# Transposing the MLP's rows by DMA instead of on TensorE, two blocks ahead, and preparing the recurrence's first operands a block earlier

## The chip, the cores and the metric

The kernel runs on one core of a Trainium2 chip. The metric is the device time of one execution in microseconds (us), the median of several. The engines named below are TensorE (PE; PEld is its weight load), VectorE (DVE), ScalarE (ACT), GpSimd (POOL) and SyncE (SP), which issues most DMAs. Each runs its own instructions in order and waits for others by semaphores.

## What is computed

Two parts share the input `x` (2048 rows of 512, bf16) and are mixed by a gate. Part A is attention over segments of 32 rows with 8 memory rows that each segment passes on to the next, so its 64 segments are a chain. Part B is a layer norm and an MLP (512 to 1376 to 512) on each row.

```
g = sigmoid((x * gate_w).sum(-1))
# A, for each segment s of 32 rows, H = 32 heads of 128:
h = concat([mem, x[s]]);  q, k, v = h @ Wq, h @ Wk, h @ Wv
o = softmax(mask(q @ k.T * scale)) @ v @ Wo;  mem = o[:8];  a[s] = o[8:]
# B:
y = (x - mean) / sqrt(var + eps)
b = gelu(y @ w1 + b1) @ w2 + b2
return g * a + (1 - g) * b
```

## The kernel before

The kernel is written under a manual schedule: each engine executes its instructions in the order in which the program emits them, and the tile framework adds the waits. A tile of a pool with `bufs=n` takes the buffer of the n-th tile before it, and its first write waits until all readers of that one are done, also those that the program emits later on another engine.

The MLP comes first (about the first 97 us), and the loop over the 64 segments (L646) after it. The weights of part A are loaded while the MLP runs.

The MLP goes over 8 blocks (`NBLK`) of 2 x 128 rows and, in each, over 11 chunks of the hidden width (`FC`). The list `units` (L504) has all (block, chunk) pairs, and the loop at L505 emits for each:

- `a_mm` (L456): four PE matmuls of a w1 chunk with the transposed rows `yT` into one of two PSUM banks (SbF and W in turn), then ACT's Gelu (L461) out of that bank into `hTm`.
- `b_mm` (L463), two units behind (`LAG`): two PE matmuls of `hTm` with w2, which sum over the chunks in banks U[0], U[1] for even blocks and U[2], U[3] for odd ones. After the last chunk ACT scales the two sums by `omg` = 1 - g into `ct` (L473), and POOL issues their stores to `c_dr` (L476).
- between them, by the chunk number, the side work:
  - chunk 0: `gates(blk - 1)` (L447): ACT's tanh of `z_all` (L449), then on DVE `g_all` and `omg` (L450, L451). Then `prep(blk + 1)` (L414) on DVE: mean and variance of the two row tiles (L420, L421), an inverse square root by Newton steps (`rsqrt`), and the normalised rows `y` (L432), in two buffers.
  - chunks 6 and 7 (7 and 8 in block 0): `prep_tr` (L435), for one row tile each: four PE transposes of `y` into bank X1 or X2 (L439), and a DVE copy to `yT` (L440).
  - chunk 7 (8 in block 0): `gate_sums` (L442) on DVE: the sums of x * gate_w of the block's two tiles into `z_all`. It is the last reader of the row tiles `xt`.
  - chunk 8: `loads(blk)` (L339) on SP: two tiles of x, which take the buffers that `gate_sums(blk)` frees (6 buffers), then two pieces of 1 MB of Wv, Wq or Wk. In block 3 it also loads `xT` of the first two tiles, by a transposing DMA from DRAM (L94), and the memory rows `m0`. Block 6 adds Wo.
  - chunk 9: a part of the constants (`consts`, L377) on DVE.

In the last block, part A's first work is mixed in by the generator `first` (L478): PE transposes of `m0` and a DVE copy to `hT[0]`, POOL copies of the left rows of tiles 0 and 1 (`left_x`, L97, into `GL`) and of `hT[0]` (`prep_h`, L235), and then 24 units of projection matmuls that read `GL` (`left_v`, `left_qk`). The numbers at L534 say how many steps of it each chunk takes.

What stands in an engine's order ahead of what matters below. On ACT: the Gelu of a(b,0), the tanh of block b-1, the Gelu of a(b,1), the two `ct` of block b-1, the Gelu of a(b,2). On POOL: the stores of `ct`, then, in the last block, `GL`. On SP: the x tiles, then the weight pieces.

Of the kernel before, what the change touches and what calls it, by code (L numbers as in the profile page):

```python
# [10 lines left out]
BF16 = mybir.dt.bfloat16  # L11
# [16 lines left out]
def kernel(ctx, tc, A_x, A_mem0, A_Wq, A_Wk, A_Wv, A_Wo, A_seg_len, B_x, B_w1, B_b1, B_w2, B_b2, gate_w, out):  # L28
    nc = tc.nc
    P = 128  # L30
    _, S, Dm = A_x.shape
# [6 lines left out]
    KC = Dm // P  # L38
# [8 lines left out]
    RIDE = 32 - M  # L47
# [23 lines left out]
    hT = [ep.tile([P, KC, 32], BF16, name=f"hT{i}") for i in range(3)]  # L71
# [20 lines left out]
    def load_xT(T):  # L92
        xT = ew.tile([P, KC, P], BF16, tag="xT", bufs=3, name="xT")
        nc.sync.dma_start_transpose(out=xT[:], in_=x2[T * P:(T + 1) * P, :])  # L94
        xTs[T] = xT

    def left_x(T):  # L97
        GL = ew.tile([P, KC, LEFT, SPT], BF16, tag="GL", name="GL")
        nc.gpsimd.tensor_copy(out=GL[:].rearrange("p k c i -> p k i c"), in_=xTs[T][:].rearrange("p k (i t) -> p k i t", i=SPT)[:, :, :, RIDE:seg])
        GLs[T] = GL  # L100
# [56 lines left out]
    dve_q, act_q = [], []  # L157

    def flush(q, n=1):
        for _ in range(min(n, len(q))):  # L160
            q.pop(0)()
# [4 lines left out]
    def left_qk(T, t, hf, bk):  # L166
        for kc in range(KC):
            qk_unit(bk, gl(T), t, hf, kc)
            if kc < KC - 1:
                yield  # L170
        def ca():
            Tb = qk_cast(bk[:])
            dve_q.append(lambda: qk_tr(Tb, QL[T % 2], hf) if t == 0 else kl_tr(Tb, T, hf))
        act_q.append(ca)
        yield
# [6 lines left out]
    def left_v(T, vb, bk):  # L182
        if vb == 0:
            VLs[T] = ew.tile([P, 4, 2, Dh], BF16, tag="VL", bufs=1, name="VL")
        for kc in range(KC):
            v_unit(bk, gl(T), vb, kc)
            if kc < KC - 1:
                yield

        def ca():  # L190
            VL = VLs[T]
            nc.scalar.copy(out=VL[:, :, vb, :], in_=bk[:].rearrange("p (a e) -> p a e", a=4))

            if vb == 1:
                vp_load(T, 0)
        act_q.append(ca)
        yield
# [37 lines left out]
    def prep_h(s):  # L235
        T, si = divmod(s, SPT)
        nc.gpsimd.tensor_copy(out=hT[s % 3][:, :, 0:RIDE], in_=xTs[T][:, :, seg * si:seg * si + RIDE])
# [54 lines left out]
    with tc.tile_pool(name="mlpw", bufs=1) as mlpw, \  # L292
         tc.tile_pool(name="mwork", bufs=2) as mwork, \
         tc.tile_pool(name="msmall", bufs=2) as msmall:
        TB = 2
        NBLK = NT // TB
# [9 lines left out]
        def ld_x(T, eng=nc.sync):  # L306
            xt = mwork.tile([P, Dm], BF16, tag="xt", bufs=6, name="xt")
            eng.dma_start(xt[:], x2[T * P:(T + 1) * P, :])
            xts[T] = xt

        def ld_w(W_, A, n):
            nc.sync.dma_start(W_[:, n, :], A[n * P:(n + 1) * P].rearrange("p h e -> p (h e)"))

        def ld_o(i):
            nc.sync.dma_start(Wo_sb[:, i:i + 8, :], A_Wo[i:i + 8].rearrange("h e d -> e h d"))
# [23 lines left out]
        def loads(blk):  # L339
            if 2 * blk + 7 < NT:  # L340
                ld_x(2 * blk + 6)
                ld_x(2 * blk + 7)
            if blk == 3:
                for T in range(2):
                    load_xT(T)
                nc.sync.dma_start(m0[:], A_mem0[0])

            for kc in range(2 * blk, min(2 * blk + 2, 3 * KC)):
                ld_w(*((Wv_sb, A_Wv), (Wq_sb, A_Wq), (Wk_sb, A_Wk))[kc // KC], kc % KC)
            if blk == 6:  # L350
                for i in range(0, H, 8):
                    ld_o(i)
# [49 lines left out]
        def rsqrt(y, v, n):  # L402
            i1 = msmall.tile([P, n], I32, tag="i1", name="i1")
            nc.vector.tensor_scalar(out=i1[:], in0=v.bitcast(I32), scalar1=1, scalar2=None, op0=ALU.logical_shift_right)
            nc.vector.tensor_scalar(out=y.bitcast(I32), in0=i1[:], scalar1=-1, scalar2=RSQRT_SEED, op0=ALU.mult, op1=ALU.add)
            for _ in range(3):
                t = msmall.tile([P, n], FP32, tag="nt", name="nt")
                nc.vector.tensor_tensor(out=t[:], in0=y, in1=y, op=ALU.mult)
                nc.vector.scalar_tensor_tensor(out=t[:], in0=t[:], scalar=-0.5, in1=v, op0=ALU.mult, op1=ALU.mult)
                nc.vector.scalar_tensor_tensor(out=y, in0=t[:], scalar=1.5, in1=y, op0=ALU.add, op1=ALU.mult)  # L410

        ys, yTs = {}, {}

        def prep(blk):  # L414
            mv = msmall.tile([P, TB, nc.vector.BN_AGGR_DIM], FP32, tag="mv", name="mv")
            ve = msmall.tile([P, TB], FP32, tag="ve", name="ve")
            rs = msmall.tile([P, TB], FP32, tag="rs", name="rs")
            for tt in range(TB):
                st = msmall.tile([P, nc.vector.BN_STATS_DIM], FP32, tag="st", name="st")
                nc.vector.bn_stats(out=st[:], in_=xts[blk * TB + tt][:])  # L420
                nc.vector.bn_aggr(out=mv[:, tt, :], in_=st[:])  # L421
            nc.vector.tensor_scalar(out=ve[:], in0=mv[:, :, 1], scalar1=LN_EPS, scalar2=None, op0=ALU.add)
            if blk == 0:
                nc.scalar.activation(out=rs[:], in_=ve[:], func=ACTF.Sqrt)
                nc.scalar.activation(out=dummy[:], in_=ident[:, 0:1], func=ACTF.Gelu_apprx_tanh)
                nc.vector.reciprocal(out=rs[:], in_=rs[:])
            else:
                rsqrt(rs[:], ve[:], TB)
            for tt in range(TB):
                T = blk * TB + tt  # L430
                ys[T] = mwork.tile([P, Dm], BF16, tag="y", name="y")
                nc.vector.tensor_scalar(out=ys[T][:], in0=xts[T][:], scalar1=mv[:, tt, 0:1], scalar2=rs[:, tt:tt + 1], op0=ALU.subtract, op1=ALU.mult)  # L432
            yTs[blk] = mwork.tile([P, KC, TB * P], BF16, tag="yT", name="yT")

        def prep_tr(blk, tt):  # L435
            y, bk = ys.pop(blk * TB + tt), (X1, X2)[tt]
            tp = bk[:].bitcast(BF16)[:, 0:Dm].rearrange("p (k t) -> p k t", k=KC)
            for kc in range(KC):
                nc.tensor.transpose(tp[:, kc, :], y[:, kc * P:(kc + 1) * P], ident[:])  # L439
            nc.vector.tensor_copy(out=yTs[blk][:, :, tt * P:(tt + 1) * P], in_=tp)  # L440
# [34 lines left out]
                        nc.vector.tensor_scalar(out=ct[:], in0=bp(blk, tt)[:], scalar1=omg[:, T:T + 1], scalar2=None, op0=ALU.mult)  # L475
                    (nc.gpsimd if blk < NBLK - 1 else nc.sync).dma_start(c_dr[T * P:(T + 1) * P, :], ct[:])  # L476

        def first():  # L478
            m0p = X1[:].bitcast(BF16)[:, 0:KC * M].rearrange("p (k m) -> p k m", k=KC)
            for kc in range(KC):  # L480
                nc.tensor.transpose(m0p[:, kc, :], m0[:, kc * P:(kc + 1) * P], ident[:M, :M])
            dve_q.append(lambda: nc.vector.tensor_copy(out=hT[0][:, :, RIDE:32], in_=m0p))
            for T in range(2):
                left_x(T)
            prep_h(0)
            yield
            bks = (X1, X2, U[0], X1, X2, U[0])
            for n, (v, t, hf) in enumerate(((1, 0, 0), (1, 0, 1), (0, 0, 0), (0, 1, 0), (0, 0, 1), (0, 1, 1))):
                yield from (left_v(0, hf, bks[n]) if v else left_qk(0, t, hf, bks[n]))
# [15 lines left out]
        for n, (blk, fc) in enumerate(units):  # L505
            a_mm(blk, fc)
            if n == len(units) - 1:
                dummy = msmall.tile([P, 1], FP32, tag="dummy", name="dummy")
                nc.scalar.activation(out=dummy[:], in_=omg[:, 0:1], func=ACTF.Exp)
            if n >= LAG:  # L510
                b_mm(*units[n - LAG])
            if fc == 0:
                if blk >= 1:
                    gates(blk - 1)
                if blk + 1 < NBLK:
                    prep(blk + 1)
                else:
                    gate_sums(blk)
            if blk + 1 < NBLK:
                f0 = 7 if blk == 0 else 6  # L520
                if fc in (f0, f0 + 1):
                    prep_tr(blk + 1, fc - f0)
                if fc == f0 + 1:
                    gate_sums(blk)
                if fc == 8:
                    loads(blk)
                if fc == 9:
                    next(cgen, None)
            elif fc >= 1:
                if fc == 1:  # L530
                    side0 = first()
                if fc == 3:
                    gates(blk)
                for _ in range((0, 1, 1, 0, 0, 8, 0, 8, 0, 8, 0)[fc]):  # L534
                    next(side0, None)
                    flush(act_q, 9)
                    flush(dve_q, 9)
# [363 lines left out]
```

## Time and profile before

| what | value |
|---|---|
| median of 3 runs | 787.48 us (785.29 to 788.54) |
| the profiled execution | 785.75 us, span 784.0 us |
| granted TensorE clock | 0.998 |
| HBM read and written | 56.96 MB and 4.45 MB |
| DMA, mean over the span | 90 GB/s |
| TensorE idle for POOL's `GL` (L99) in the last block | 1.5 us |

The span is the time from the first to the last instruction of the profile; the execution's own time is 1.75 us longer. Busy time of an engine counts each instruction from start to end; PE's matmuls overlap, so that the distance from one start to the next is what a matmul costs. Rows of a timeline give start, duration, engine, line, operation, output and inputs, the number of instructions merged, and in brackets the idle time before and what ended it.

### The profile page before, as it was taken

The page shows a single profiled execution, that of the slowest core. Times are in us where ns is not written, and L with a number is a line of the kernel's source. Part 1 is how long each engine was busy: PE and PEld are TensorE (multiplying, and loading weights), DVE is VectorE, ACT ScalarE, POOL GpSimd, SP SyncE. Part 2 cuts the span into 40 slices and gives each one's busy share as a digit, 9 for nine tenths or more (in the row PEclk, how much of TensorE's full clock was granted, in tenths as well). Part 3 has the DMA queues.
Part 4 walks back from the last instruction along what each step waited for, and adds up shares of the span by engine and source line. Part 5 has one row for each costly group of instructions (what it writes and reads, how often), then busy time and mean ns, then how long its engine had stood idle before and what let it go on. Part 6 is the DMA issues. An engine that isn't in the chain of part 4 may idle for free.

```text
span 784.0 us, 44302 instructions
## 1 busy us (share of the span) xinstructions
PE 766.3 (98%) x19673; PEld 416.6 (53%) x19687; DVE 341.2 (44%) x1235; ACT 524.5 (67%) x1439; POOL 278.8 (36%) x523
## 2 busy tenths in 40 slices
PE   7999999999999999999999999999999999999996
PEld 5666455555555555555555555555555555555553
DVE  5776244334334343434443433434343444434334
ACT  4666566667677676667667677766666767666663
POOL 4111034333344343344434424443334443342342
PEclk9999999999999999999999999999999999999999
DMA  6789311213121222212121212122221212221211
GB/s 199 271 256 387 119 57 61 74 61 88 61 61 62 78 71 77 72 58 74 49 88 61 88 62 74 60 67 70 78 72 57 80 43 88 62 80 62 67 63 44
DMA packets 53174, 70.61 MB, mean 90 GB/s; under 512 B 21289, under 2 KB 42898, under 8 KB 51442
## 3 DMA queue, kind: packets, MB, share of 16 engines
q1 hardware_dynamic: 51250, 64.84, 25.6%
q8 instruction: 156, 2.56, 1.3%
q0 software_dynamic: 784, 1.97, 0.7%
q10 hardware_dynamic: 944, 0.92, 0.4%
q14 instruction: 40, 0.33, 0.1%
HBM read 56.96 MB, written 4.45 MB: 78 GB/s over the span
## 4 chain that ended last, share of the span: by engine, by line
PE 87%; DVE 1%; issue 0%; ACT 0%; DVEq 0%
PE U L120 30%; PE X L139 18%; PE W L151 15%; PE X L120 7%; PE X L151 4%; PE U L281 3%; PE U L640 2%; PE U L268 1%; PE W L257 1%; PE SbF L257 1%; PE W L249 1%; PE SbF L600 1%; PE SbF L249 1%; PE U L286 1%; PE U L466 1%; PE U L221 0%
## 5 line engine op out<-in xcount | busy, mean ns | idle before, releaser
L626 POOL TENSOR_TENSOR UT<-XR,Rb 128x384 bf16<-128x384 bf16 x126 | 140.3, 1134 | 297.6 <-DMA Rb<-r_dr 237.6
L125 ACT CAST Tb<-U 128x512 bf16<-128x512 f32 x258 | 150.9, 585 | 86.6 <-PE U L120 85.6
L120 PEld LDWEIGHTS <-hT 128*32 128x32 bf16 x4096 | 98.3, 96 | 110.9 <-DVE hT L642 26.8
L139 PE MATMUL X<-Wv_sb,hT 128*32 128x512 bf16 x2048 | 145.7, 379 | 0.0
L120 PE MATMUL U<-Wq_sb,hT 128*32 128x512 bf16 x2048 | 139.9, 381 | 0.8 <-DVE hT L642 0.5
L120 PE MATMUL U<-Wk_sb,hT 128*32 128x512 bf16 x2048 | 132.7, 379 | 0.0
L151 PE MATMUL W<-Wo_sb,UT 128*32 128x512 bf16 x2080 | 124.8, 380 | 1.5 <-ACT UT L718 1.5
L642 DVE CAST hT<-U 128x16 bf16<-128x16 f32 x126 | 22.0, 175 | 222.7 <-PE U L640 222.4
L129 DVE STREAM_TRANSPOSE QT<-Tb 128x256 f32<-128x256 f32 x128 | 56.6, 443 | 78.4 <-ACT Tb L125 78.4
L151 PEld LDWEIGHTS <-UT 128*32 128x32 bf16 x2080 | 57.8, 96 | 57.7 <-issue 18.5
L606 ACT CAST XR<-U 128x256 bf16<-128x256 f32 x252 | 78.6, 438 | 0.0
L129 DVE STREAM_TRANSPOSE KT<-Tb 128x256 f32<-128x256 f32 x128 | 57.1, 446 | 44.5 <-ACT Tb L125 44.3
L633 ACT CAST w<-W 128x256 bf16<-128x256 f32 (+1 forms) x128 | 41.9, 378 | 46.5 <-PE W L151 46.5
L139 PEld LDWEIGHTS <-hT 128*32 128x32 bf16 x2048 | 53.1, 95 | 20.4
L618 POOL TENSOR_TENSOR racc<-racc,R 128x72 f32<-128x72 f32 x63 | 21.2, 336 | 111.7 <-PE U L286 79.3
L626 POOL TENSOR_TENSOR UL<-XR,Rb 128x128 bf16<-128x128 bf16 x126 | 60.3, 502 | 0.0
L718 ACT CAST UT<-U 128x64 bf16<-128x64 f32 x252 | 35.3, 227 | 28.3 <-PE U L286 28.3
L710 ACT CAST V<-X 128x512 bf16<-128x512 f32 x64 | 37.4, 585 | 22.3 <-PE X L139 22.1
L466 PE MATMUL U<-w_sb,hTm 128*128 128x512 bf16 (+1 forms) x163 | 49.2, 379 | 0.6
L696 ACT CAST V<-X 128x512 bf16<-128x512 f32 x64 | 37.4, 585 | 15.6 <-PE X L139 15.6
L460 PEld LDWEIGHTS <-w_sb 128*128 128x128 bf16 (+1 forms) x352 | 34.2, 101 | 20.3 <-issue 3.0
L640 PEld LDWEIGHTS <-w 128*32 128x32 bf16 x1008 | 20.7, 94 | 42.6 <-ACT w L633 29.3
(158 smaller groups left out, 1179.8 us busy)
## 6 DMA issues: line engine op xcount, KB each, us to landing
Rb<-r_dr SPq DMA_DIRECT2D x63, 512.0 KB, 3.8
Wv_sb<-in_A_Wv_dram SPq DMA_DIRECT2D x4, 1024.0 KB, 6.5
Wq_sb<-in_A_Wq_dram SPq DMA_DIRECT2D x4, 1024.0 KB, 7.0
Wk_sb<-in_A_Wk_dram SPq DMA_DIRECT2D x4, 1024.0 KB, 9.5
Wo_sb<-in_A_Wo_dram SPq DMA_DIRECT2D x4, 1024.0 KB, 15.0
VP<-VL SPq DMA_DIRECT2D x64, 64.0 KB, 3.2
c<-c_dr SPq DMA_DIRECT2D x16, 128.0 KB, 3.3
out_dram<-o SPq DMA_DIRECT2D x16, 128.0 KB, 2.1
```

The source lines that it names most:

```text
L120: nc.tensor.matmul(bk[32 * j:32 * j + 32, :], lhsT=G[:, kc, :], rhs=W5[t][:, kc, h0:h1, j, :], start=(kc == 0), stop=(kc == KC - 1), tile_ ...
L125: nc.scalar.copy(out=Tb[:], in_=bk.rearrange("p (a b e) -> p a e b", a=8, b=2))
L129: nc.vector.transpose(out=dst[:, 8 * hf:8 * hf + 8, c0:c0 + 32, :].rearrange("p a r b -> p a (r b)").bitcast(FP32), in_=Tb[:].rearrange("p ...
L139: nc.tensor.matmul(bk[32 * j:32 * j + 32, :], lhsT=G[:, kc, :], rhs=Wv5[:, kc, 4 * vb:4 * vb + 4, j, :], start=(kc == 0), stop=(kc == KC - ...
L151: nc.tensor.matmul(bk[32 * c:32 * c + 32, :], lhsT=U_[:, j, i, :], rhs=Wo_sb[:, 4 * i + j, :], start=(n == 0), stop=(n == NW - 1), tile_po ...
L466: nc.tensor.matmul(bp(blk, tt)[:], lhsT=hTm[blk % 2][:rows, fc, tt * P:(tt + 1) * P], rhs=w2_sb[:rows, fc, :], start=(fc == 0), stop=(fc = ...
L606: nc.scalar.copy(out=XR[:, j], in_=U[j][:, 0:NG * 40].rearrange("p (i q) -> p i q", q=40)[:, :, 0:32])
L626: nc.gpsimd.tensor_tensor(out=out[:, :, 4 * h:4 * h + 4, o:o + b - a], in0=XR[:, :, 4 * h:4 * h + 4, a:b], in1=Rb[:, h, :, :, a:b], op=ALU ...
L633: nc.scalar.copy(out=w[:, a:a + Dm // parts], in_=W[:, a:a + Dm // parts])
L640: nc.tensor.matmul(bk[32 * c:32 * c + 32, M * k:M * k + M], lhsT=w[:, k * P + 32 * c:k * P + 32 * c + 32], rhs=SelM[:], start=(k == k0), s ...
L696: nc.scalar.copy(out=v_out(V, 0), in_=X1[:])
L710: nc.scalar.copy(out=v_out(V, 1), in_=X2[:])
```

## The change

For blocks 2 to 7, `yT` is no longer made by PE transposes and a DVE copy. SP issues a transposing DMA for each row tile, from `y` in SBUF to `yT` in SBUF (`dma_tr`). For this `prep` runs two blocks ahead: `prep(1)` at chunk 0 of block 0 and `prep(2)` at its chunk 8, ahead of `gate_sums(0)`; from block 1 on `prep(blk + 2)` at chunk 0. `dma_tr` of block 2 stands at chunks 1 and 3 of block 1, that of blocks 3 to 7 at chunk 7 of the block two before, ahead of `gate_sums` and `loads`. `yT` gets a third buffer; `y` keeps two. Blocks 0 and 1 keep the PE transposes.

The beginning of `first` (transposes of `m0`, `GL` of two tiles, `hT[0]`) becomes a function `first_h`, called at chunk 4 of block 6, with the DVE copy at once. `first` begins with the projection matmuls, and the numbers of steps for chunks 1 and 2 become 0.

```
             else:
                 rsqrt(rs[:], ve[:], TB)
+            yTs[blk] = mwork.tile([P, KC, TB * P], BF16, tag="yT", bufs=3, name="yT")
             for tt in range(TB):
...
-            yTs[blk] = mwork.tile([P, KC, TB * P], BF16, tag="yT", name="yT")
+
+        def dma_tr(blk, tt):
+            nc.sync.dma_start_transpose(out=yTs[blk][:, :, tt * P:(tt + 1) * P], in_=ys.pop(blk * TB + tt)[:])
...
-        def first():
+        def first_h():
             m0p = X1[:].bitcast(BF16)[:, 0:KC * M].rearrange("p (k m) -> p k m", k=KC)
             for kc in range(KC):
                 nc.tensor.transpose(m0p[:, kc, :], m0[:, kc * P:(kc + 1) * P], ident[:M, :M])
-            dve_q.append(lambda: nc.vector.tensor_copy(out=hT[0][:, :, RIDE:32], in_=m0p))
+            nc.vector.tensor_copy(out=hT[0][:, :, RIDE:32], in_=m0p)
             for T in range(2):
                 left_x(T)
             prep_h(0)
-            yield
+
+        def first():
             bks = (X1, X2, U[0], X1, X2, U[0])
...
-                if blk + 1 < NBLK:
-                    prep(blk + 1)
-                else:
+                if blk == 0:
+                    prep(1)
+                elif blk + 2 < NBLK:
+                    prep(blk + 2)
+                elif blk + 1 == NBLK:
                     gate_sums(blk)
             if blk + 1 < NBLK:
-                f0 = 7 if blk == 0 else 6
-                if fc in (f0, f0 + 1):
-                    prep_tr(blk + 1, fc - f0)
-                if fc == f0 + 1:
+                if blk == 0 and fc in (7, 8):
+                    prep_tr(1, fc - 7)
+                if 0 < blk and blk + 2 < NBLK and fc == 7:
+                    for tt in range(TB):
+                        dma_tr(blk + 2, tt)
+                if blk == 0 and fc == 8:
+                    prep(2)
+                if blk == 1 and fc in (1, 3):
+                    dma_tr(2, (fc - 1) // 2)
+                if fc == (8 if blk == 0 else 7):
                     gate_sums(blk)
                 if fc == 8:
                     loads(blk)
+                if blk == NBLK - 2 and fc == 4:
+                    first_h()
                 if fc == 9:
                     next(cgen, None)
...
-                for _ in range((0, 1, 1, 0, 0, 8, 0, 8, 0, 8, 0)[fc]):
+                for _ in range((0, 0, 0, 0, 0, 8, 0, 8, 0, 8, 0)[fc]):
```

## The prediction

> **What bounds the kernel now.** I read the page first, then the engines in order of time over the first 100 us, where the MLP and the whole change lie.
>
> ```profile
> span 784.0 us, 44302 instructions
> PE 766.3 (98%) x19673; PEld 416.6 (53%) x19687; DVE 341.2 (44%) x1235; ACT 524.5 (67%) x1439; POOL 278.8 (36%) x523
> POOL c_dr L476 <- ACT ct L473: 66.4, 7, 12.3
> PE X L139 <- POOL GL L99: 1.5, 1, 1.5
> ```
>
> TensorE is busy for 98% of the span, so only what TensorE does, or waits for, counts. The last row, from the waits of the first 100 us, is its one long wait there. The profiled execution took 785.75 us, the median shown is 787.48; I work in the first and add the difference in time to the second. About 0.5% (3.9 us) is what a measurement of this kernel can tell from no change. Below, a(b,f) is `a_mm` of block b, chunk f.
>
> **What goes.** Block 2 starts at 28.43, block 3 at 38.56, with two groups of PE transposes (L439) between them.
>
> ```profile
> 24.08 0.59 PE L466 MATMUL U<-w_sb,hTm 128*128 128x512 bf16 x2
> 24.51 0.39 PE L439 MATMUL X<-ident,y 128*128 128x128 bf16 x4
> 24.73 0.60 PE L460 MATMUL SbF<-yT,w_sb 128*128 128x256 bf16 x4
> ...
> 28.43 0.60 PE L460 MATMUL SbF<-yT,w_sb 128*128 128x256 bf16 x4
> ...
> 31.48 0.59 PE L466 MATMUL U<-w_sb,hTm 128*128 128x512 bf16 x2
> 32.04 0.60 PE L460 MATMUL SbF<-yT,w_sb 128*128 128x256 bf16 x4
> ...
> 38.56 0.60 PE L460 MATMUL W<-yT,w_sb 128*128 128x256 bf16 x4
> ...
> 81.56 0.59 PE L466 MATMUL U<-w_sb,hTm 128*128 128x512 bf16 x2
> 83.68 0.40 PE L139 MATMUL X<-Wv_sb,GL 128*32 128x512 bf16 x4 [1.53 <-POOL GL L99]
> 84.01 0.61 PE L460 MATMUL SbF<-yT,w_sb 128*128 128x256 bf16 x4
> ```
>
> ```profile
> 82.00 1.12 POOL L476 DMA_DIRECT2D c_dr<-ct  x2 [9.02 <-ACT ct L473]
> 83.16 0.75 POOL L99 COPY GL<-xT 128x128 bf16<-128x128 bf16 x2
> ```
>
> (1) A group of four transposes moves the next matmul from 24.51 to 24.73: 0.22 us. Six blocks with two groups each: 12 x 0.22 = **2.64 us less**. A block goes from 10.13 to 9.69. The DVE copies (L440) go too, but DVE isn't the bound.
>
> (2) The pair at 81.56 takes 0.43 from start to start (as 24.08 to 24.51), so PE could go on at 81.99 and does at 83.68: 1.69. It waits for GL, whose copies stand on POOL behind the two stores of ct. Moved to block 6, chunk 4, the copies have some ten us before the first V matmul needs them. The four V matmuls join a longer run of their kind (about 0.1 less), and a wait of 0.13 ahead of a(b,4) (31.48 + 0.43 against 32.04; step 3 says what it is), which the gap covers in block 7 today, comes back there. The four m0 transposes cost PE the same earlier. Sum: 1.69 + 0.1 - 0.13 = **1.7 us less**.
>
> **What is added: a wait in block 1.** `prep(2)` now stands on DVE ahead of `gate_sums(0)`. Three engines around the start of block 1 (18.36):
>
> ```profile
> 16.82 0.42 DVE L440 COPY yT<-X 128x512 bf16<-128x512 bf16 x1 [0.67 <-PE X L439]
> 17.16 0.68 DVE L445 SCALAR_TENSOR_TENSOR junk<-xt,gw_bc 128x512 bf16<-128x512 bf16 x1
> ...
> 18.51 0.08 DVE L445 DVE_READ_ACCUMULATOR junk<-xt,gw_bc 128x1 f32 x1
> ...
> 19.66 0.16 DVE L450 TENSOR_SCALAR g_all<-th 128x2 f32<-128x2 f32 x1
> 19.73 0.16 DVE L451 TENSOR_SCALAR omg<-th 128x2 f32<-128x2 f32 x1
> 19.80 0.69 DVE L420 BATCH_NORM_STATS2 st<-xt 128x6 f32<-128x512 bf16 x1
> ...
> 23.95 0.73 DVE L432 TENSOR_SCALAR y<-xt,mv,rs 128x512 bf16<-128x512 bf16 x2
> ```
>
> ```profile
> 19.37 0.19 ACT L449 ACTIVATE th<-z_all 128x2 f32<-128x2 f32 x1
> 19.86 0.47 ACT L461 ACTIVATE hTm<-SbF,b_sb 128x256 bf16<-128x256 f32 x1 [0.30 <-PE SbF L460]
> 20.23 1.26 ACT L473 ACTIVATE ct<-U,omg 128x512 bf16<-128x512 f32 x2
> 21.37 0.48 ACT L461 ACTIVATE hTm<-W,b_sb 128x256 bf16<-128x256 f32 x1
> ```
>
> ```profile
> 20.96 0.60 PE L460 MATMUL SbF<-yT,w_sb 128*128 128x256 bf16 x4
> 21.40 0.59 PE L466 MATMUL U<-w_sb,hTm 128*128 128x512 bf16 x2
> 21.91 0.60 PE L460 MATMUL W<-yT,w_sb 128*128 128x256 bf16 x4
> ```
>
> (3) A `prep` takes 19.80 to 24.68 = 4.88 on DVE. All DVE rows from 17.16 on move by that: z of block 0 is ready at 18.59 + 4.88 = 23.47, the first constants and g_all follow, omg ends at 19.89 + 4.88 = 24.77. The tanh (L449) sits in ACT's order ahead of Gelu(1,1); behind Gelu(1,1) come the two ct, which need omg, and Gelu(1,2). So: tanh 23.5, Gelu(1,1) 23.6 to 24.1, ct from 24.8, Gelu(1,2) 1.14 later (as 20.23 to 21.37), 25.94 to 26.42. `a_mm` has two banks: a(1,3) waits for Gelu(1,1), a(1,4) for Gelu(1,2). Today a(1,4) starts 0.06 after that Gelu ends (21.85, 21.91; the 0.13 of other blocks is the same wait). It will start at 26.47: **4.56 us more**. PE idles 3.2 us before a(1,3) and 1.5 before a(1,4). Nothing covers this: PE has no other work in its order. Block 2 can then start at 28.43 + 4.56 - 0.44 = 32.55.
>
> The clock matters here: after the idle start of the kernel the same four matmuls took 1.03, later 0.60.
>
> ```profile
> 8.16 1.03 PE L460 MATMUL SbF<-yT,w_sb 128*128 128x256 bf16 x4
> ...
> 11.83 0.60 PE L460 MATMUL SbF<-yT,w_sb 128*128 128x256 bf16 x4
> ```
>
> The Trainium skill, "TensorE: Matmul & The Clock Gate", Part 1, says that an idle window of about 3.4 us halves the array's clock until a busy one has passed. By that the stall, split 3.2 and 1.5, is on the edge, and an estimate from the page's window is up to 1.7 us on top; the 1.5 us gap of today left no slow matmul (0.61 at 84.01). I leave it out of the sum.
>
> **What is added: transposes on SP's queue.**
>
> ```profile
> 18.62 0.33 SPq L308 DMA_DIRECT2D xt<-in_A_x_dram  x1
> 19.00 0.90 SPq L312 DMA_DIRECT2D Wv_sb<-in_A_Wv_dram  x2
> ...
> 48.46 2.61 SPq L94 DMA_TRANSPOSE xT<-in_A_x_dram  x2
> ```
>
> ```profile
> 27.71 0.23 DVE L389 TENSOR_SCALAR Mk<-iof,rf 128x24 bf16<-128x24 f32 x1
> ...
> 28.19 0.23 DVE L392 TENSOR_SCALAR Mk<-Mk,mk 128x8 bf16<-128x8 bf16 x1
> ```
>
> ```profile
> DMA to landing us min/median/max: 5.8/7.2/8.7
> DMA to landing us min/median/max: 2.9/3.4/4.0
> DMA to landing us min/median/max: 1.9/3.0/7.4
> ```
>
> The two DVE rows are the first and last of the four constants that follow a `gate_sums`. The landing rows are: the first two Wv loads, the two xT transposes at 48.46, all loads of x. No run before transposes from SBUF; the xT rows (DRAM source, same shape) are the nearest, and I take them.
>
> (4) SP's x(6), x(7) and Wv issues wait for `gate_sums(0)` and move by 4.88 too; Wv goes out at 23.88 to 24.78, the two transposes of block 2 behind it until 27.4, in the same queue. The second Wv is issued at 24.33; I let it land 8.0 later, between the row's 7.2 and the 8.7 that this very load took, and the transposes 1 us behind it: yT(2) at 33.4. PE is ready at 32.55: **0.8 more**. Bounds: nothing (5.8 and 1 give 31.1), or 3.4 (8.7 and a whole 2.9 behind it give 35.9).
>
> (5) `prep(3)` writes y into the two buffers that these transposes read. The write, ready at about 29, waits for the landings (32.9, 33.4); behind it on DVE stand `gate_sums(1)` (1.42, so 35.2), four constants (27.71 to 28.42, 0.7) and omg: 36.1. Block 2's ct would want omg 1.94 after its start (in the rows of step 3: 20.23 is 1.87 after 18.36), at 35.3: **0.8 more**, through the same chain as in step 3.
>
> (6) From then on DVE and SP go round in a loop: y ready, two transposes issued (2.61), then x for the block after (SP's order; 0.1), landed (3.0, the median), statistics to the first y (19.80 to 23.95 = 4.15), y (0.4): 10.26 a block against PE's 9.69. Once late it stays late: 0.5 + 0.6 + 0.6 in blocks 3 to 5, and 0.25 in block 6, where no constants follow: **1.95 more**. Bounds: with 1.9 for x the loop takes 9.2 and catches up, nothing; at 3.5 or with slower issues (0.5 more per block) 3.9.
>
> The Trainium skill, "Advanced Engine Details and Errata", "X-Bar Transpose (TRN2)", has transposing DMAs as fast as regular ones. The rows differ: 1.3 us of issue against 0.33 for x of the same bytes, 3.4 to land against 1.9 to 3.0. By the page's rule the loop would be 8.3, step 6 nothing and the sum +1.9.
>
> **Sum**: 4.56 + 0.8 + 0.8 + 1.95 - 2.64 - 1.7 = **+3.8 us**: 789.5 for the profiled execution, 791.3 for the median. What follows the MLP only starts later. SP now holds the last weights back until the y of block 7 are ready; they aren't read before the recurrent part, so I cost that at nothing (late weights would show as PE waiting for a DMA there). `gate_sums` of blocks 1 to 6 stays at chunk 7, and one `prep` a block stays on DVE.
>
> **Rivals.**
> A. *The gates don't wait*: if the tanh were not held by `gate_sums(0)`, steps 3 to 6 vanish and the gain comes whole: -4.3, 783.1. Against it: in the rows above, DVE and ACT run strictly in program order, and the tanh reads z. Chance 0.05.
> B. *Only block 1 stalls*: Wv lands in 5 to 7 us, yT(2) is on time, and the loop, starting without delay, has 1.6 us of slack in block 3. Then 4.56 - 4.3 = +0.2, 787.7 (with step 4 alone +1.0). For it: x has landed in as little as 1.9. Against: the 8.7 of exactly this Wv pair. Chance 0.24.
> C. *The loop is the bound, heavily*: a transpose from SBUF issued in 1.8 instead of 1.3, or x held up behind the transposes. The loop is then 11.2, so blocks 3 to 6 lose 1.4 each instead of 0.5, +7.4, 794.9; it decides as soon as the loop exceeds the old 10.13, for then each later block is slower than before. For it: the queue stands near full behind two weight loads. Chance 0.16, the clock's drop included.
>
> **How the numbers follow.** My forecast 0.55, with a range of its own of +2 to +6 (789.5 to 793.5), which straddles the bound of +3.9 evenly: 0.27 same, 0.28 slower. B is "same" but for 0.01, C is slower. So faster 0.06, same 0.50, slower 0.44. The range leaves out A and the far half of C: 787.0, just under B, to 796.0.
>
> **What would show it.** Right: in block 1 a PE gap of about 3 us and one of 1.5, both ended by ACT, and ACT idle until DVE L445; the tanh at 23.5; no L439 after block 0's second group; GL before 76; no wait on GL; DVE waiting at L432 in block 1 for a transpose; block starts at 18.36, 33.4, 43.9, 54, 64 and later about 10.2 apart. Block starts 9.69 apart from block 2 on prove B; over 10.8 apart, C. The forecast is wrong at its root if a(1,3) starts before 22.

## The result, and the profile after

The kernel after takes 794.53 us in the median of 6 runs (792.44 to 797.82), the kernel before beside it 786.99 (785.29 to 788.54). The ratio is **1.0095, 95% interval 1.0081 to 1.0110: slower**, by some 7.5 us. 791.3 was predicted, with a range of 787 to 796. The profiled execution after took 794.55 us.

Read first where the time lies. The stretches of each kernel, cut at the block starts on PE (first row: from block 0's first matmul to block 1; then block 1, blocks 2 to 5, block 6, block 7 with the recurrent part up to the loop's first mask matmul, L249, and the rest). Columns: start and end, length, busy time with the number of instructions of PE, PEld, DVE, ACT, POOL, then the granted clock, the DMA share and GB/s. Before:

```profile
8.16:18.36 10.20, 9.98 (x70) 6.97 (x72) 6.33 (x24) 4.96 (x11) 0.69 (x3) 1.00 0.61 190
18.36:28.43 10.07, 10.02 (x75) 6.93 (x74) 8.41 (x40) 6.23 (x15) 1.11 (x2) 1.00 0.77 272
28.43:68.96 40.53, 40.22 (x292) 27.79 (x296) 28.57 (x116) 24.86 (x57) 4.32 (x8) 1.00 0.83 290
68.96:79.09 10.13, 10.08 (x74) 6.95 (x74) 6.70 (x26) 6.23 (x15) 1.08 (x2) 1.00 1.05 375
79.09:97.58 18.49, 16.80 (x170) 8.83 (x171) 4.14 (x16) 10.92 (x23) 1.90 (x5) 1.00 0.35 112
97.58:784.00 686.42, 674.91 (x18966) 355.33 (x18966) 283.40 (x1005) 468.09 (x1318) 262.43 (x462) 1.00 0.22 68
```

After:

```profile
8.26:19.50 11.24, 11.24 (x72) 7.55 (x71) 6.32 (x24) 4.96 (x11) 0.63 (x3) 1.00 0.54 170
19.50:36.32 16.82, 12.55 (x67) 7.45 (x66) 11.22 (x51) 6.34 (x15) 1.11 (x2) 0.80 0.56 174
36.32:75.07 38.75, 38.75 (x266) 26.00 (x265) 22.50 (x100) 24.87 (x57) 4.32 (x8) 1.00 0.96 275
75.07:88.94 13.87, 11.49 (x72) 7.04 (x71) 5.18 (x22) 6.34 (x15) 1.90 (x5) 0.88 0.87 305
88.94:105.44 16.50, 16.50 (x167) 8.85 (x165) 4.04 (x15) 10.79 (x23) 1.08 (x2) 1.00 0.77 252
105.44:792.80 687.36, 675.11 (x18967) 354.89 (x18966) 283.12 (x1005) 468.25 (x1318) 262.25 (x462) 1.00 0.22 68
```

The length column gives the differences: start +1.14 (with the 0.10 by which block 0 starts later), block 1 **+6.75**, blocks 2 to 5 -1.78, block 6 **+3.74**, block 7 -1.99, the rest +0.94; together +8.80, the difference of the spans (792.8 against 784.0). The clock column shows more: 0.80 in block 1 and 0.88 in block 6, 1.00 in every other row. Both costly blocks hold a stall and then a slower clock. (The column doesn't show everything: the first groups of block 0 take 1.03 in both kernels, at 8.16 and 8.26, and its row says 1.00.)

Block 1 on PE, after:

```profile
21.68 0.59 PE L469 MATMUL U<-w_sb,hTm 128*128 128x512 bf16 x2
25.14 0.60 PE L463 MATMUL SbF<-yT,w_sb 128*128 128x256 bf16 x4 [2.87 <-ACT hTm L464]
25.57 0.59 PE L469 MATMUL U<-w_sb,hTm 128*128 128x512 bf16 x2
27.57 1.01 PE L463 MATMUL W<-yT,w_sb 128*128 128x256 bf16 x4 [1.40 <-ACT hTm L464]
28.38 1.06 PE L469 MATMUL U<-w_sb,hTm 128*128 128x512 bf16 x2
...
33.28 0.59 PE L469 MATMUL U<-w_sb,hTm 128*128 128x512 bf16 x2
...
36.32 0.60 PE L463 MATMUL SbF<-yT,w_sb 128*128 128x256 bf16 x4
```

The two gaps are those of step 3: ahead of a(1,3) and a(1,4), ended by ACT. a(1,4) starts 8.07 after the block; before it was 3.55 (18.36 to 21.91): **4.52 lost in the stall**. From 27.57 on six groups take 1.01 to 1.06 and a seventh 0.81, instead of 0.60. The seven groups from 27.57 to 33.28 take 5.71; at the rate of the next seven (33.28 to 36.32, 0.434 each) they would take 3.04. So **2.67 is lost to the clock**. 4.52 + 2.67 - 0.44 (no transposes) is the whole +6.75.

The chain behind the gaps, on DVE and on ACT, after:

```profile
23.06 0.68 DVE L448 SCALAR_TENSOR_TENSOR junk<-xt,gw_bc 128x512 bf16<-128x512 bf16 x1
...
25.63 0.16 DVE L454 TENSOR_SCALAR omg<-th 128x2 f32<-128x2 f32 x1
...
34.49 0.80 DVE L433 TENSOR_SCALAR y<-xt,mv,rs 128x512 bf16<-128x512 bf16 x2 [4.36 <-DMA yT<-y]
```

```profile
24.52 0.20 ACT L452 ACTIVATE th<-z_all 128x2 f32<-128x2 f32 x1 [3.91 <-DVE junk L448]
25.89 1.26 ACT L476 ACTIVATE ct<-U,omg 128x512 bf16<-128x512 f32 x2 [0.80 <-DVE omg L454]
```

The tanh waits 3.91 for the gate sums, ct another 0.80 for omg. The third DVE row is step 5's wait: y of `prep(3)` stands 4.36 for the transposes that read its buffer. But PE is then still in block 1, held there by the clock, and nothing comes of it in block 2 (e2 shows what came of it later).

Block 6 on PE, and what it waited for, after:

```profile
77.24 0.59 PE L469 MATMUL U<-w_sb,hTm 128*128 128x512 bf16 x2
79.54 0.60 PE L463 MATMUL W<-yT,w_sb 128*128 128x256 bf16 x4 [1.70 <-ACT hTm L464]
...
81.25 1.01 PE L463 MATMUL SbF<-yT,w_sb 128*128 128x256 bf16 x4 [0.68 <-ACT hTm L464]
82.06 1.06 PE L469 MATMUL U<-w_sb,hTm 128*128 128x512 bf16 x2
...
84.59 0.60 PE L463 MATMUL SbF<-yT,w_sb 128*128 128x256 bf16 x4
```

```profile
72.69 0.69 DVE L420 BATCH_NORM_STATS2 st<-xt 128x6 f32<-128x512 bf16 x1 [5.75 <-DMA xt<-in_A_x_dram]
...
78.81 0.08 DVE L448 DVE_READ_ACCUMULATOR junk<-xt,gw_bc 128x1 f32 x1
```

```profile
78.92 0.20 ACT L452 ACTIVATE th<-z_all 128x2 f32<-128x2 f32 x1 [2.68 <-DVE junk L448]
```

It is the same chain, released later by another cause: statistics on DVE wait 5.75 for a load of x, so `gate_sums(5)` ends at 78.81, the tanh waits, and a(6,4) starts 81.25 - 75.07 = 6.18 after the block instead of 3.61 (28.43 to 32.04 before): 2.57. The four steps to 84.59 and the m0 transposes among them take 3.34; in e3, at the full clock, the same take 2.02 (74.05 to 76.07): 1.32 for the clock, and 2.02 - 4 x 0.434 = 0.28 for the m0 transposes. Why x came late stands on SP's queue, after:

```profile
58.61 2.50 SPq L94 DMA_TRANSPOSE xT<-in_A_x_dram  x2
61.15 0.48 SPq L346 DMA_DIRECT2D m<-in_A_mem_dram  x1
61.69 1.90 SPq L312 DMA_DIRECT2D Wq_sb<-in_A_Wq_dram  x2
64.58 2.62 SPq L436 DMA_TRANSPOSE yT<-y  x2
67.29 1.03 SPq L308 DMA_DIRECT2D xt<-in_A_x_dram  x2
```

```profile
xt<-in_A_x_dram SPq DMA_DIRECT2D x2, 128.0 KB, 5.2
```

The first view is SP's order, the second the issues from 67.0 to 68.4 with the median time to landing. The two xT transposes push Wq back, and the yT transposes go out right behind it (they took 7.2 to land; on a quiet queue 2.4 to 2.5). x is issued behind all that and lands after 5.2, where step 6 had 3.0.

### The profile page after: what moved, and what is told of

Same layout as the page of the kernel before. It is cut to its first block, busy times and chain, and to the rows that moved or that the text cites. A ratio compares the mean times of both kernels' runs of the same rounds, so it can differ in the third digit from the quotient of the medians.

```text
span 792.8 us, 44239 instructions
## 1 busy us (share of the span) xinstructions
PE 769.9 (97%) x19639; PEld 415.6 (52%) x19639; DVE 335.9 (42%) x1223; ACT 524.7 (66%) x1439; POOL 278.7 (35%) x523
## 4 chain that ended last, share of the span: by engine, by line
PE 91%; DVE 4%; DMA 3%; ACT 1%; issue 1%; POOL 0%; SPq 0%; ACTq 0%; DVEq 0%; POOLq 0%
PE U L120 29%; PE X L139 18%; PE W L151 14%; PE X L120 7%; PE X L151 4%; PE U L281 3%; PE U L469 3%; PE W L463 2%; PE U L654 2%; PE SbF L463 2%; PE U L268 1%; DMA xt<-in_A_x_dram 1%; PE W L257 1%; PE SbF L614 1%; PE W L249 1%; PE SbF L257 1%
## 5 line engine op out<-in xcount | busy, mean ns | idle before, releaser
L469 PE MATMUL U<-w_sb,hTm 128*128 128x512 bf16 (+1 forms) x176 | 54.5, 394 | 0.0
L463 PEld LDWEIGHTS <-w_sb 128*128 128x128 bf16 (+1 forms) x352 | 36.1, 105 | 32.3 <-issue 12.4
```

Source lines behind the costliest of these rows:

```text
L463: nc.tensor.matmul(hp[:rows, 0:TB * P], lhsT=w1_sb[:, kc, fc * P:fc * P + rows], rhs=yTs[blk][:, kc, :], start=(kc == 0), stop=(kc == KC - 1))
L469: nc.tensor.matmul(bp(blk, tt)[:], lhsT=hTm[blk % 2][:rows, fc, tt * P:(tt + 1) * P], rhs=w2_sb[:rows, fc, :], start=(fc == 0), stop=(fc = ...
```

## The experiments

Each ratio is to the kernel before, run beside it, with its 95% interval. "MLP" is the stretch from a(1,0) to the loop's first mask matmul in the profiled execution: 79.22 before (18.36 to 97.58), 85.94 after (19.50 to 105.44). It leaves out the start of the kernel, which varies by itself (last section).

| kernel | ratio | MLP, us |
|---|---|---|
| after | 1.0095 (1.0081 to 1.0110) | 85.94 |
| e8, before + `prep(2)` early | 1.0074 (1.0061 to 1.0088) | 86.43 |
| e1, after + gate sums first | 1.0055 (1.0038 to 1.0073) | 80.76 |
| e2, after + four y buffers | 1.0048 (1.0035 to 1.0061) | 81.81 |
| e4, after + filled gaps | 1.0080 (1.0064 to 1.0096) | 85.52 |
| e5, after + xT loads later | 1.0072 (1.0059 to 1.0085) | 81.98 |
| e3, before + `first_h` | 0.9984 (0.9974 to 0.9994) | 77.64 |
| e6, one block ahead | 1.0037 (1.0023 to 1.0051) | 81.18 |
| e7, e6 + xT loads first | **0.9972 (0.9961 to 0.9983)** | 75.47 |

**e8_prep2_only: is the early `prep(2)` enough?** The kernel before, with `prep(2)` moved ahead of `gate_sums(0)` and nothing else.

```
             if fc == 0:
...
-                    prep(blk + 1)
+                    if blk != 1:
+                        prep(blk + 1)
...
+                if blk == 0 and fc == 8:
+                    prep(2)
                 if fc == f0 + 1:
                     gate_sums(blk)
```

> The kernel before with one edit: prep(2) stands in block 0, ahead of gate_sums(0), and not in block 1; PE transposes everywhere, nothing by DMA, first operands as before. Theory: this alone makes the stall of block 1, 4.5 us in two gaps before chunks 3 and 4, and the half clock after it (0 to 2.7 by where the stall falls in the clock's window); later blocks run at 10.13 as before: 4.5 to 7.2 more than before, most likely 6 (1.0057 to 1.009). Rival: the stall needs the transposes on SP's queue: under 2 us (1.0025).

PE in block 1 of this kernel:

```profile
25.43 0.60 PE L460 MATMUL SbF<-yT,w_sb 128*128 128x256 bf16 x4 [2.87 <-ACT hTm L461]
25.86 0.59 PE L466 MATMUL U<-w_sb,hTm 128*128 128x512 bf16 x2
27.86 1.01 PE L460 MATMUL W<-yT,w_sb 128*128 128x256 bf16 x4 [1.40 <-ACT hTm L461]
```

Gaps of 2.87 and 1.40, to the hundredth those of the kernel after, and the same slow groups behind them. The time rises by 0.74%, some 5.8 us. Nothing of the transposing DMA is in this kernel: the order of two pieces of DVE work costs more than half a per cent by itself. Block 1 is 7.2 us longer in the profiled execution, of which 4.52 is stall and the rest, 2.69, the clock; the interval of the time ends at 6.9, which suggests that other executions lost less to the clock.

**e1_sums_first: the mirror image.** The kernel after, with `gate_sums(0)` back ahead of `prep(2)`.

```
-                if blk == 0 and fc == 8:
-                    prep(2)
...
                 if fc == (8 if blk == 0 else 7):
                     gate_sums(blk)
+                if blk == 0 and fc == 8:
+                    prep(2)
```

> Block 0's gate sums stand ahead of prep(2) on DVE, all else as in the changed kernel. Theory: the stall of block 1 has two links, the tanh behind z and the ct behind omg, and prep(2) still stands ahead of omg. Then the wait for the tanh (2.87 us of PE before chunk 3) goes, but chunk 4 waits as before for the ct: one gap of about 4.3 us in place of 2.9 and 1.4, the clock drops again, 794.5 (793 to 796). Rival: only the sums hold up the tanh, and so the stall is that one wait: 794.5 - 4.5 - 2.7 for the clock, about 787 to 790.

```profile
28.35 1.01 PE L463 MATMUL W<-yT,w_sb 128*128 128x256 bf16 x4 [4.43 <-ACT hTm L464]
```

```profile
20.91 0.90 SPq L312 DMA_DIRECT2D Wv_sb<-in_A_Wv_dram  x2
```

The first row is PE, the second SP. The tanh is free, so a(1,3) is on time; omg still stands behind `prep(2)` in DVE's order, ct waits for it, and the one gap falls ahead of a(1,4) with 4.43, about as long as the two gaps together; a(1,4) starts 8.07 after the block, as in the kernel after. That is step 3's chain with both of its links. The time was missed: it falls by 0.4% against the kernel after. The swap frees SP too: x and Wv wait for the gate sums, and Wv goes out 0.63 after the start of block 1 (20.28) instead of 5.39 (24.89 after 19.50). All that follows on the queue is earlier: DVE has no wait for yT left, and block 6 takes 10.09 instead of 13.87. Of the 5.18 that the MLP gains, 3.78 is block 6; the other 1.40 is a shorter slow stretch behind the stall in block 1. So the early `prep` cost twice, once on ACT's chain and once through SP's queue, and the prediction had the first and, of the second, only what it does to block 2.

**e2_four_y: step 5 undone.**

```
-                ys[T] = mwork.tile([P, Dm], BF16, tag="y", name="y")
+                ys[T] = mwork.tile([P, Dm], BF16, tag="y", bufs=4, name="y")
```

> Four buffers for y in place of two, all else as in the changed kernel. Theory: DVE no longer waits 4.4 us in block 1 for the transposes to read y, the gate sums of block 1 end about 4.4 earlier, so x for block 4 is asked for earlier and the loop of DVE, SP and x gets about 2 us of room back. The stall in block 6 (3.9 us with its clock drop) shrinks to under 1: 791.2 (790.5 to 792.5). The stall in block 1 stays. Rival: block 6 stalls because x(14) lands late behind the weights, whatever came before: 794.5.

```profile
24.47 0.89 PE L463 MATMUL SbF<-yT,w_sb 128*128 128x256 bf16 x4 [2.87 <-ACT hTm L464]
...
26.90 1.01 PE L463 MATMUL W<-yT,w_sb 128*128 128x256 bf16 x4 [0.69 <-ACT hTm L464]
...
34.50 0.60 PE L463 MATMUL SbF<-yT,w_sb 128*128 128x256 bf16 x4 [0.81 <-DMA yT<-y]
...
77.77 0.60 PE L463 MATMUL SbF<-yT,w_sb 128*128 128x256 bf16 x4 [0.68 <-ACT hTm L464]
```

The time falls by 0.47% against the kernel after, some 3.7 us, close to what was expected. The stall of block 1 stays (8.07), DVE's 4.36 at y is gone, and with it most of block 6's stall (4.54 instead of 6.18, where 3.61 is undisturbed). The wait for the y buffers cost nothing where the prediction put it, and about 1.6 four blocks later. The clock fell at the first gap here: two slow groups lie inside the stall, where a(1,4) had to wait anyway, and only the two behind it cost time, 0.54 (26.90 to 28.31 instead of 2 x 0.434). So step 4 comes into sight: block 2 waits 0.81 for yT(2). 0.8 had been predicted, but that the two agree is in part luck: yT(2) was to come 15.0 after a(1,0) and came 15.67 after it, and PE was ready later too.

**e4_warm: the gaps filled.** 50 and 25 matmuls of the identity into an unused bank ahead of a(1,3) and a(1,4); they add nothing to the output.

```
+            for _ in range({(1, 3): 50, (1, 4): 25}.get((blk, fc), 0)):
+                nc.tensor.matmul(X2[:, 0:P], lhsT=ident[:], rhs=ident[:], start=True, stop=True, skip_group_check=True)
             a_mm(blk, fc)
```

> 50 and 25 matmuls of the identity into an unused bank ahead of chunks 3 and 4 of block 1, where PE stands idle, all else as in the changed kernel; they add nothing to the result. They keep the array busy, so the clock should stay: no matmul group of 1.0 us after the stall. Theory: the 2.7 us of half clock were partly cover: block 2 then waits for the transposed rows instead (some 1.2 us), and what is left (1.4) is taken back in block 6, whose gate sums come at the pace of DVE and x: 794.5 (793.5 to 795). Rival: the clock's loss adds up, 794.5 - 2.7 = 791.8.

```profile
35.77 1.01 PE L463 MATMUL SbF<-yT,w_sb 128*128 128x256 bf16 x4 [2.25 <-DMA yT<-y]
...
39.13 0.60 PE L463 MATMUL SbF<-yT,w_sb 128*128 128x256 bf16 x4
```

No slow group follows the stall, so the idle time is what lowered the clock. But blocks 1 and 2 together gain nothing (27.73 instead of 26.51): PE now waits 2.25 for yT(2) at block 2, and the clock falls there (four groups in 3.36 instead of 1.74). The clock's 2.67 and step 4 cover each other; they don't add. The interval of the time (1.0064 to 1.0096) overlaps that of the kernel after and can't tell this from a small gain; the traces carry the reading.

**e5_xT_late: block 6's cause.** The xT loads moved from block 3's loads to the end of block 4's.

```
             if blk == 3:
-                for T in range(2):
-                    load_xT(T)
...
+            if blk == 4:
+                for T in range(2):
+                    load_xT(T)
```

> The two transposing loads of xT from DRAM go out in block 4 behind the weights instead of block 3 ahead of them, all else as in the changed kernel. Theory: in block 3 they hold SP for 2.5 us, the weights behind them run into the transposes and x of the next block, and x(14) takes 5.2 us to land. Without them the weights finish 2.5 earlier, x(14) lands in about 3, the gate sums of block 5 end at about 76.3 instead of 78.8, and block 6 stalls under 0.5 with no clock drop: 790.9 (790 to 792). Rival: the issue of two transposes a block and the landing of x make the loop slower than PE anyway: 794 to 794.5.

```profile
71.15 0.69 DVE L421 BATCH_NORM_STATS2 st<-xt 128x6 f32<-128x512 bf16 x1 [3.89 <-DMA xt<-in_A_x_dram]
```

```profile
79.71 0.60 PE L464 MATMUL SbF<-yT,w_sb 128*128 128x256 bf16 x4 [0.68 <-ACT hTm L465]
```

DVE waits 3.89 for x instead of 5.75, and block 6's stall falls from 2.57 to 0.80 with no slow group. The MLP gains 3.96, but the time only some 1.8 by the ratios, and their intervals overlap: half of what was expected, at most a hint in the time itself. Not all of the 3.96 is the edit's: block 6 gives 3.10 (10.77 instead of 13.87), and 1.33 comes from block 1, where the clock fell for four groups only behind the same stall. Blocks 2 and 4 became 0.24 and 0.22 longer.

**e3_first_h_only: step 2 alone**, on the kernel before: `first_h` split off and called at chunk 4 of block 6.

```
-        def first():
+        def first_h():
...
+                if blk == NBLK - 2 and fc == 4:
+                    first_h()
```

> The kernel before with the second part of the change alone: the beginning of the recurrence's first operands moved to block 6, chunk 4, PE transposes kept everywhere. Theory: the wait for GL in block 7 goes and nothing takes its place, 1.7 us less than before (785.3 where before is 787.0; 784.8 to 785.8). Rival: the copies collide with the stores of ct on POOL or with PE's banks in block 6, no gain (787).

```profile
80.97 0.60 PE L460 MATMUL W<-yT,w_sb 128*128 128x256 bf16 x4
...
84.58 0.60 PE L460 MATMUL W<-yT,w_sb 128*128 128x256 bf16 x4
```

a(7,4) is 3.61 behind a(7,0), as in the undisturbed blocks; the wait for GL, 1.53 before, is gone. The MLP gains 1.58 (block 7 takes 1.99 less, block 6 0.40 more, of which 0.28 is the m0 transposes), the time 0.16%, some 1.3 us. This half of the change is a small gain.

**e6_one_ahead: another order.** Both parts of the change, but `prep` one block ahead and cut in two: `prep_a` (statistics, L420 and L421 before) at chunk 3 for the block two ahead, `prep_b` (the rest) at chunk 0 behind the gates; then the gate sums, then transposes, then loads. yT keeps two buffers, the xT loads go to the end of block 4, and weights are spread anew.

```
+                elif blk + 1 < NBLK:
+                    prep_b(blk + 1)
...
+                    if fc == 1:
+                        gate_sums(blk)
+                    if fc == 2:
+                        for tt in range(TB):
+                            dma_tr(blk + 1, tt)
+                        loads(blk)
+                    if fc == 3 and blk + 2 < NBLK:
+                        prep_a(blk + 2)
```

> Both parts of the change with another order: the statistics of a block's rows (the mean and variance only) on DVE at the end of the block two ahead, the rest of the normalisation behind the gates of the block one ahead, its DMA transposes at once, and SP's order in each block: transposes, x, weights; the weights run one block later, xT goes out in block 4. yT has two buffers as before. Theory: it was the order on DVE and SP, not transposing by DMA, that cost the time: with the gates never behind a whole normalisation and the transposes ahead of the weights, no wait of PE on ACT or DMA over 0.3 us from block 1 to 6, and 2.6 and 1.7 come off: 4.3 less than before, 782.7 where before is 787.0 (782 to 784). Rival: transposing DMAs beside the weight loads are late wherever they stand, PE waits for yT or ACT by a us or more a block: 787 or more.

On SP, and on PE, of this kernel:

```profile
56.48 0.90 SPq L312 DMA_DIRECT2D Wq_sb<-in_A_Wq_dram  x2
57.42 0.43 SPq L312 DMA_DIRECT2D Wk_sb<-in_A_Wk_dram  x1
57.90 7.17 SPq L94 DMA_TRANSPOSE xT<-in_A_x_dram  x2
65.17 3.68 SPq L447 DMA_TRANSPOSE yT<-y  x2
```

```profile
71.09 0.60 PE L474 MATMUL SbF<-yT,w_sb 128*128 128x256 bf16 x4 [3.54 <-DMA yT<-y]
```

Block 1 is free of stalls (18.60 to 28.22, 9.62). But it is slower than the kernel before all the same: behind three weights the two xT transposes hold SP for 7.17, the yT transposes of block 6 wait behind them, and PE stands 3.54 (with a slow stretch behind it). Here the order on the queue decides, not the engines.

**e7_xT_first: the queue cleared.** e6 with the xT loads in block 0's loads, when no weights are in front of them, and two weights a block.

```
+            if blk == 0:
+                for T in range(2):
+                    load_xT(T)
...
-            for kc in range(*((0, 0), (0, 2), (2, 4), (4, 6), (6, 9), (9, 12), (0, 0))[blk]):
+            for kc in range(2 * max(blk - 1, 0), 2 * blk):
...
-            if blk == 4:
-                for T in range(2):
-                    load_xT(T)
```

> As the run one_ahead, but xT and m0 are loaded in block 0, before any weight, and two weight pieces go out in each of the blocks 1 to 6 (there it was three in blocks 4 and 5 with xT behind them, and PE waited 3.5 us at block 6 and 0.5 at block 7 for yT). Theory: those waits were transposes queued behind three weights and xT; they go, blocks 1 to 6 take 9.7 each, and the time is 4.3 less than before less some 0.7 for a wait of ACT at the start of the segments: 0.9955 of before (0.994 to 0.9975). Rival: the transposes still come late behind two weights in blocks 5 to 7: no faster than before (0.998 or more).

```profile
39.70 0.60 PE L473 MATMUL W<-yT,w_sb 128*128 128x256 bf16 x4 [0.45 <-DMA yT<-y]
```

This is the only wait over 0.3 left on PE in blocks 1 to 7; the MLP takes 75.47, 3.75 less than before, of which 0.87 is given back in the loop's first turn (see the end of the next section). The kernel takes 783.99 us against 786.47: **faster than the kernel before**, by 0.28%, and so than the kernel after too; 0.45% was the forecast. In the trace its MLP is 2.17 shorter than that of e3, which has step 2 alone, so step 1 adds its share; in the time the intervals of e7 and e3 overlap, and the share of step 1 isn't shown there. The change spent both gains, and more, on its order.

## Why the prediction was right or wrong

The time lies within the range, 3.2 above the forecast; "slower" had been given 0.44, "same" 0.50. The forecast's main term was right; of the rest, three terms were absent and others stood in their place. That the time fell inside the range is in part luck: steps 4 to 6 were to bring 3.55 and brought 2.57, in another block; the clock, left out, brought 3.99; and the upper end of the range came from rival C, whose 794.9 holds no term for the clock.

| term | predicted | measured in the trace |
|---|---|---|
| step 1, transposes gone | -2.64 | -2.64 (blocks of 9.69 instead of 10.13) |
| step 2, `first_h` moved | -1.7 | -1.71 (block 7 -1.99, block 6 +0.28); -1.58 in e3 |
| step 3, stall in block 1 | +4.56 | +4.52 |
| step 4, yT(2) late | +0.8 | 0 (covered); 0.81 in e2, 2.25 in e4 |
| step 5, block 2's ct late | +0.8 | 0 (covered) |
| step 6, the loop | +1.95 | 0 in blocks 2 to 5, +2.57 in block 6 |
| clock | left out | +2.67 and +1.32 |
| start; rest | 0; 0 | +1.14; +0.94 |

- **Step 3 held** to 0.04, place and chain included: reading three in-order engines side by side around one block start was enough. e8 shows that this order alone makes the stall, e1 that both links exist.
- **The step that failed is the one on the clock**: "I leave it out of the sum." The price named beside it, up to 1.7, was also too small: 2.67 in block 1, and 1.32 more in block 6, where no stall had been foreseen. The Trainium skill, "TensorE: Matmul & The Clock Gate", Part 1, gives an idle window of about 3.4 us as the condition, and calls the window free-running: it doesn't start anew with a kernel. Here gaps of 2.87 and 1.40 with 0.9 of work between them were enough, in e2 the 2.87 alone, and in e4 a single one of 2.25; the 1.53 of before was not. So the measured gaps are shorter than the page's figure. That the same 2.87 was followed by slow groups at once in e2 and not in the kernel after, and that the loss behind the like stall varied (2.67 after, 1.34 in e5, 0.54 in e2), agrees with a free-running window, but no run here shows the window itself.
- **Steps 4 and 5 didn't come as losses**: the wait on DVE is there (4.36), but the clock kept PE in block 1 until 36.32. With the clock full in e4, step 4 cost 2.25, inside its bounds of 0 to 3.4, though the transposes also came later there: y of `prep(3)`, which waits for them, starts 16.05 after a(1,0) in e4 and 14.99 in the kernel after. Step 5 was never seen without cover and stays untested as a loss of PE.
- **Step 6 was right that x behind transposes is the weak spot, wrong on where.** Blocks 2 to 5 are 9.69 apart, the mark set for rival B. PE was late enough from block 1 that the loop had slack, and it lost that slack only at the xT loads, which the prediction had in its rows (48.46) and didn't follow to the block that they would reach. Step 6 held x at 3.0; the load that counted took 5.2. e5 and e2, which take off one delay each, shrink that stall to 0.80 and 0.93.
- **Rivals.** A fell. B described blocks 2 to 5, but not block 6. C gave 794.9, near the time, yet not by its mechanism: no block from 2 to 5 is slower than before. Its condition "x held up behind the transposes" came true once, ahead of block 6.
- **The start**, +1.14, is hardly the change's: over the ten profiled executions a(1,0) lies between 18.36 and 20.60, and the one before is the earliest. Without it the trace gives +7.66, which fits the 7.5 of the runs.
- **The rest**, +0.94, holds one new wait of 0.74 on PE in the loop's first turn, for an ACT instruction that waits 1.0 for the small DMA `VP<-VL`. The last weights (Wo) were costed "at nothing". The wait (0.19 to 0.87) is in six of the seven kernels with transposing DMAs, whose Wo issues end 7 to 14 us before the loop, and in none of before, e3 and e8, where they end over 16 us before it; but e4 has no such wait with 12. That late weights make it is therefore likely and not shown. The rest takes 687.2 to 687.9 in the five executions with a wait of 0.4 or more and 684.7 to 686.7 in the other five, so part of the 0.94 may be chance.

## What to carry to other kernels

When a block of work is moved forward in the program, list on every engine and every DMA queue what now stands behind it, and price the first consumer of each: here a `prep` of 4.88 us put ahead of two small sums cost more than twelve groups of transposes gave. Transposing by DMA paid here, by the trace, once nothing large stood in front of it on its queue (e7); so move the large loads first, then the work. And the stall of a few microseconds on TensorE brought a second bill, the clock, of up to 2.7; it belongs in the sum or in the range.

## What the runs showed of the hardware

- **The clock fell after shorter idle times than the prediction expected.** After single gaps of 2.25 (e4), 2.87 (e2), 3.54 (e6) and 4.43 (e1), and after 2.87 + 1.40 (after, e5, e8) or 1.70 + 0.68 (after, block 6), matmul groups took 1.01 to 1.06 instead of 0.60. The slow stretch lasted 3.0 to 5.7 us and began at once or up to 0.9 after the gap (e6: 71.09 and the group behind it are still fast). Gaps of 0.81 (e2), 1.53 (before) and 1.38 + 0.68 (e4, block 6) left no slow group. Work in the gap (e4's 75 small matmuls) prevented it.
- **The start of a kernel isn't repeatable to a microsecond.** Before and e3 differ only from block 6 on, yet a(1,0) starts at 18.36 in the one and 19.83 in the other: the slow groups at the beginning go on for longer or shorter.
- **A DMA's issue can hold its engine's queue.** Two xT transposes took 2.50 us of SP behind x alone and 7.17 behind three weights (e6); in the kernel after a transpose from SBUF took 1.2 to 1.8 of issue and, where the profile gives it, landed 2.4 to 7.2 us later, the 7.2 behind two weight loads. The Trainium skill, "Advanced Engine Details and Errata", "X-Bar Transpose (TRN2)", calls transposing DMAs as fast as regular ones: the trace agrees for the landing on a quiet queue (2.4 to 2.5 against 2.0 for the quickest x), not for the issue (1.2 at the least against 0.5 at the most for x).
